# How the softmax denominators reach DRAM and come back: blocks of 32x32 transposed on VectorE, 128-byte rows, and the broadcast and the multiply in later groups

## The chip, the cores and the metric

The kernel runs on one core of one Trainium2 chip. The metric is the device time of one execution in microseconds. Before the change three runs gave 1148.82, 1153.21 and 1153.7 us (median 1153.21).

## The reference

Attention over 4 batches of 8 heads (576 tokens, head size 64), with a threshold in the softmax, then two feed-forward layers over the 2304 tokens:

```python
scores = scale * np.matmul(q, k.transpose(0, 1, 3, 2))
thresh = np.max(scores, axis=-1, keepdims=True) - tau
scores = np.where(scores >= thresh, scores, -1000000000.0)
scores = scores - np.max(scores, axis=-1, keepdims=True)
attn = np.exp(scores)
attn = attn / (np.sum(attn, axis=-1, keepdims=True) + 1e-09)
x = np.matmul(attn, v)                       # to 2304 x 512
h = x @ w_in;   x = (h * sigmoid(1.702 * h)) @ w_out
h = x @ w_in2;  out = (h * np.tanh(softplus(h))) @ w_out2
```

All inputs and the output are float32. `w_in` is 512x2048, `w_out` 2048x512.

## The kernel before

**Stages.** Attention comes first (to about 362 us), then layer 1 and layer 2, which are long rows of TensorE matmuls to the end. A "head" below is a pair of heads (b, hp), 16 of them. Each head is five groups: four "full" ones of 128 query rows for both heads of the pair, and one "mix" group of the last 64 rows of both.

**One group.** `qk` (L599) multiplies queries by keys into the score banks. `softmax_a` does the rest for each half: VectorE scales and takes the row extremum (L621), GpSimd adds the threshold to a 128x1 column `nm` (L625), ScalarE takes the exponential (L628), and VectorE masks it and sums each row into one column of the tile `sm` (L631). Two groups later (AHEAD = 2) `attend` transposes the probabilities on TensorE (L691, and L686 for the tail), ScalarE copies them to SBUF (L702), TensorE multiplies them with the values (L716), and ScalarE copies the product, still without its denominator, into the head's tile `xo` (L723). The L716 matmuls of a mix group are 64 columns wide, those of a full one 128; that is how heads are told apart in the trace.

**The denominators.** After the mix group `scale_x` takes the nine columns of `sm` (128 partitions x 9), inverts them on VectorE (L644), stores them to a DRAM row `r_d` of 1152 numbers in which the partition runs fastest (L645), reads that row back three times, broadcast over 64 partitions each, into the one tile `rb` (L648), multiplies `xo` by `rb` on GpSimd (L654) and stores the result to `x_d` (L656), from where layer 1 loads it. The store and the loads are

```python
dma(lambda: nc.sync.dma_start(out=rd.rearrange("(j q) -> q j", q=128), in_=sums), ...)
dma(lambda: nc.sync.dma_start(out=rb[rows:rows + 64, c0:c0 + m],
    in_=rd[at:at + m].rearrange("(o q) -> o q", o=1).to_broadcast([64, m])), ...)
```

**What sets the order.** Every operation is given to a planner (`Order.add`) with an engine, an estimated duration, the tiles it reads and writes, and a rank. `Order.run` simulates the engines with a list scheduler (lowest rank first among what is ready) and emits the program in the order of the simulated times. So each engine, and SP, which issues all DMAs, runs a fixed order in which every instruction waits for its own data, with all that is behind it waiting too. The planner takes a DMA to need 2.0 us and its bytes at 200 GB/s (L21, L22), whatever its shape. Operations marked `port` on VectorE and GpSimd are planned one at a time.

**Beside it.** From group 40 on (the eighth head of the sixteen has gone by) one block of layer 1's weights is loaded in each head (`sr`, L371 and L375; blocks 0 to 7 in the attention stage, 8 to 15 behind it) and split by `conv_w` and `split_w` into a high and a low part: three ScalarE operations (L380, L382, L400), four on VectorE (L386, L389, L394, L402) and one on GpSimd (L392). Keys and values of coming heads are loaded by L576 and L577 on SP. Layer 1's matmuls are L495 and L540, layer 2's L495 and L885.

Of the kernel before, what the change touches and what calls it, by code (L numbers as in the profile page):

```python
# [11 lines left out]
F32 = mybir.dt.float32  # L12
# [3 lines left out]
ALU = mybir.AluOpType  # L16
# [7 lines left out]
AR = 0.1  # L24
# [9 lines left out]
AHEAD = 2  # L34
# [166 lines left out]
def attention_then_two_ffn_kernel(  # L201
# [21 lines left out]
    nc = tc.nc  # L223
    B, HP, _, S = kq.shape
    S = S // 2
# [88 lines left out]
    def t_tt(n):  # L314
        return 0.15 + n * 2.1e-3

    def dma(fn, nbytes, r=(), w=(), rank=0.0, deps=(), dur=0.47):
        return add("SP", dur, fn, r, w, rank, deps, nbytes)
# [242 lines left out]
    pps = Ring(apool, "p", NP // 2, [128, P1 + S + 1], F32)  # L561
    sss = Ring(apool, "ss", NSS, [128, S + 5], F32)
    nms = Ring(apool, "nm", 4, [128, 2], F32)
    sms = Ring(apool, "sm", 2, [128, 9], F32)
    rbs = Ring(apool, "rb", 1, [128, S], F32)
    pms = Ring(apool, "pm", NPM, [128, 512], F32)
    pmt = Ring(apool, "pmt", 2, [128, 128], F32)
# [2 lines left out]
    sm = {}  # L570
# [36 lines left out]
    def softmax_a(sums, ksum, col, rank, bank, pair, i):  # L607

        s3, ksc = bank
        ns, kns = sss.next()
        at, a = (4, 3) if i == 0 else (P1, P1)
        whole = slice(a, a + S + 1)
        p, kp = pair[0], pair[1] + (i,)
        nm, kn = nms.next()
        n3 = ns[:, 4:4 + S].rearrange("p (g n) -> p g n", g=2)
        scored.append(len(sch.ops))
        add("DVE", t_dve(S) + 0.075,  # L620
            lambda: nc.vector.tensor_scalar(  # L621
                n3, s3, nqsc, None, ALU.mult, ALU.min, accum_out=nm[:, 0:1]),
            ksc, [kn, kns], rank - SMR)
        add("POOL", 0.2,
            lambda: nc.gpsimd.tensor_scalar(nm[:, 1:2], nm[:, 0:1], tau_p, 0.0, ALU.add, ALU.add),  # L625
            [kn, "qsc"], [kn + (1,)], rank - SMR, port=True)
        add("ACT", t_act(S, 1, False),
            lambda: nc.scalar.activation(p[:, at:at + S], ns[:, 4:4 + S], AF.Exp, bias=nm[:, 0:1], scale=-1.0),  # L628
            [kns, kn], [kp], rank)
        add("DVE", t_dve(S) + 0.08,  # L630
            lambda: nc.vector.scalar_tensor_tensor(  # L631
                p[:, whole], ns[:, 3 + i:4 + S + i], nm[:, 1:2], p[:, whole], ALU.is_le, ALU.mult,
                accum_out=sums[:, col:col + 1]),
            [kns, kn, kn + (1,), "qsc"], [kp, ksum + (col,)], rank, port=True)
        return kp

    def scale_x(b, hp, rank):

        sums, ksum = sm[b, hp]
        x, kx = xo[b, hp]  # L640
        rb, krb = rbs.next()
        rd = r_d[b * HP + hp]
        keys = [ksum + (i,) for i in range(9)]
        add("DVE", 0.2, lambda: nc.vector.reciprocal(sums, sums), [], keys, rank)  # L644
        n = dma(lambda: nc.sync.dma_start(out=rd.rearrange("(j q) -> q j", q=128), in_=sums),  # L645
                4608, keys, [("rd", b, hp)], rank)
        for rows, c0, at, m in ((0, 0, 0, S), (64, 0, 640, 512), (64, 512, 576, 64)):
            dma(lambda rows=rows, c0=c0, at=at, m=m: nc.sync.dma_start(  # L648
                out=rb[rows:rows + 64, c0:c0 + m],
                in_=rd[at:at + m].rearrange("(o q) -> o q", o=1).to_broadcast([64, m])),  # L650
                64 * m * 4, [("rd", b, hp)], [krb + (rows + c0,)], rank)
        kr = [krb + (i,) for i in (0, 64, 576)]
        add("POOL", t_tt(S),
            lambda: nc.gpsimd.tensor_tensor(x, x, rb, ALU.mult),  # L654
            kr, [kx + (i,) for i in range(5)], rank, port=True)
        n = dma(lambda: nc.sync.dma_start(out=x_d[1][hp, :, b * S:(b + 1) * S], in_=x),  # L656
                128 * S * 4, [kx + (i,) for i in range(5)], [], rank)
        x_stores.append((n, 1, b * S, (b + 1) * S))

    def attend(tl, ps, pair, rank):  # L660

        kind, b, hp, t = tl
        full = kind == "full"
        _, vr, _, kvr = head[b, hp]
        w = 128 if full else 64
        at = t * 128
        if t == 0:
            xo[b, hp] = xos.next()
        if full:
            plan = [(0, pms, (0, 1), 128, 512), (1, pms, (2, 3), 128, 512), (2, pmt, (4,), 128, 128)]  # L670
        else:
            plan = [(0, pms, (0, 1, 2, 3), 128, 512), (1, pmt, (4,), 64, 128)]
        where, copies, keys = {}, [], []
        for bank, ring, cs, rows, cols in plan:
            pn, kpn = ring.next()
            keys.append(kpn)
            for n, c in enumerate(cs):
                where[c] = (bank, n * 2 * w, pn)
            copies.append((bank, pn, kpn, rows, cols))

        def tr(cs):
            for c in cs:
                bank, c0, _ = where[c]
                if c == 4:
                    m = 64 * len(ps)
                    nc.tensor.transpose(tb[bank][0:m, 0:128], pair[:, 516:516 + m], ident)  # L686
                    yield
                    continue
                for i in range(len(ps)):
                    a = (P1 + 64 if i else 4) + c * 128  # L690
                    nc.tensor.transpose(  # L691
                        tb[bank][:, c0 + i * 128:c0 + (i + 1) * 128], pair[:, a:a + 128], ident)
                    yield

        for (bank, pn, kpn, rows, cols), (*_, cs, _, _) in zip(copies, plan):
            n = 1 if 4 in cs else len(ps) * len(cs)
            n = add("PE", n * 0.109 + (0.16 if bank == 0 else 0.0), lambda cs=cs: tr(cs),
                ps, [("tb", bank)], rank, steps=max(n, 2))
            if sch.fill is None and WARM:
                sch.fill = ("PE", n, 0.107, keep_warm)  # L700
            add("ACT", t_act(cols),
                lambda pn=pn, bank=bank, rows=rows, n=cols: nc.scalar.copy(pn[0:rows, 0:n], tb[bank][0:rows, 0:n]),  # L702
                [("tb", bank)], [kpn], rank)
        i = avn[0] % 2
        avn[0] += 1
        av, kav = tb[3][:, i * 128:i * 128 + w], ("tb", 3, i)

        def mm():
            for c in range(5):
                _, c0, pn = where[c]  # L710
                for i in range(2):
                    rows, at, vc = slice(0, 128), c0 + i * w, c * 128 + 64 * i
                    if c == 4:
                        rows = slice(64 * i, 64 * i + 64) if full else slice(0, 64)
                        at, vc = (0, 512) if full else (64 * i, 512 + 64 * i)
                    nc.tensor.matmul(  # L716
                        av[64 * i:64 * i + 64], vr[rows, vc:vc + 64], pn[rows, at:at + w],
                        start=(c == 0), stop=(c == 4))
                    yield

        add("PE", len(CK) * 0.107 * (2 if full else 1) + 0.2, mm, keys + [kvr], [kav], rank - AR, steps=2 * len(CK))
        x, kx = xo[b, hp]
        add("ACT", t_act(w), lambda: nc.scalar.copy(x[:, at:at + w], av), [kav], [kx + (t,)], rank - AR)  # L723
        if not full:
            scale_x(b, hp, rank - AR)

    avn = [0]


    groups = []  # L730
# [10 lines left out]
    def make_ident():  # L741
        make_identity(nc, ident)
        nc.sync.dma_start(out=tau_b, in_=tau.to_broadcast([128, 1]))
        for t in sss.tiles:
            for c in (3, S + 4):
                nc.vector.memset(t[:, c:c + 1], -3.0e38)
        for t in pps.tiles:
            for c in (3, P1 + S):
                nc.vector.memset(t[:, c:c + 1], 1e-9)
        nc.vector.tensor_scalar_max(tau_p, tau_b, 0.0)  # L750
        nc.vector.tensor_scalar(nqsc, tau_b, 0.0, -scale, ALU.is_ge, ALU.mult)
# [5 lines left out]
    for gi, tl in enumerate(groups + [None] * AHEAD):  # L757
        first = len(sch.ops)
        if tl:
            for bh in preps.get(gi, []):  # L760
                prep(*bh, gi - PR)
            kind, b, hp, t = tl
            if t == 0:
                sm[b, hp] = sms.next()
            sums, ksum = sm[b, hp]
            pair, kpair = pps.next()
            ps = [softmax_a(sums, ksum, 5 * i + t, gi, bank, (pair, kpair), i)
                  for i, bank in enumerate(qk(tl, gi))]
            marks.append(len(sch.ops) - 1)
            behind.append((tl, ps, pair, gi))  # L770
        if gi >= AHEAD:
            attend(*behind.pop(0))
        att.extend(range(first, len(sch.ops)))

    def load_w1_from(fs):
# [197 lines left out]
```

## Time and profile before

| | |
|---|---|
| runs | 1148.82, 1153.21, 1153.7 us |
| profiled execution, own time | 1149.93 us |
| its span, first to last instruction | 1147.7 us |
| mean granted TensorE clock | 0.978 of full speed |
| busy: TensorE, VectorE, ScalarE, GpSimd | 96%, 59%, 57%, 16% of the span |
| DMA, mean over the span | 82 GB/s |

The profile counts an engine as busy while an instruction is on it; a TensorE that counts as busy may run at half its clock, so the granted clock is read beside it. "Idle before" is the time in which an engine had nothing running before an instruction, with the event that ended it behind an arrow.

### The profile page before, as it was taken

Reading aid. Unit: us, or ns where it says so; the run is one execution under the profiler, and the core shown is the slowest. Engines: PE = TensorE matmul, PEld = TensorE weight load, DVE = VectorE, ACT = ScalarE, POOL = GpSimd, SP = SyncE. Lnnn points to the kernel's source line nnn. Section 1 sums busy time; section 2 is a strip of 40 time slices with the busy share of each in tenths; the row PEclk is TensorE's granted clock in tenths of the full one; section 3 lists DMA queues with packets and bytes.
Section 4 is the critical chain, followed back from the end, with each engine's and each line's share of the span. In section 5 each row is a group of like instructions: output and inputs, shape, how many; then the busy total and the mean of one; then the engine's idle time right before and its main releaser. Section 6 shows DMA issues by size and latency. Waiting matters only on the chain.

```text
span 1147.7 us, 17435 instructions
## 1 busy us (share of the span) xinstructions
PE 1102.8 (96%) x6708; PEld 887.9 (77%) x6708; DVE 678.4 (59%) x1336; ACT 651.2 (57%) x1065; POOL 183.4 (16%) x198
## 2 busy tenths in 40 slices
PE   9999998978888999999999999999999999999998
PEld 7667665655656889988888888888888888888887
DVE  7668776777776874554553334456554654554554
ACT  5657666766665644554442234468656656555665
POOL 2323323333433420230320000000000000000000
PEclk9989998989989999999999999999999999999999
DMA  2223414544448434454551033230010010000010
GB/s 86 83 78 94 105 54 123 104 134 91 93 100 166 163 104 145 169 200 147 186 175 44 2 110 106 96 129 1 28 37 1 10 37 1 1 28 10 1 38 18
DMA packets 66690, 94.51 MB, mean 82 GB/s; under 512 B 23856, under 2 KB 41776, under 8 KB 66608
## 3 DMA queue, kind: packets, MB, share of 16 engines
q1 hardware_dynamic: 66608, 93.41, 27.7%
q8 instruction: 52, 0.85, 0.3%
q14 instruction: 30, 0.25, 0.1%
HBM read 70.78 MB, written 22.62 MB: 81 GB/s over the span
## 4 chain that ended last, share of the span: by engine, by line
PE 70%; DMA 6%; DVE 1%; ACT 1%; issue 1%; SPq 0%; POOL 0%; ACTq 0%; DVEq 0%; POOLq 0%
PE h L495 34%; PE tb L885 17%; PE tb L540 17%; DMA sr<-in_w_out 5%; PE sc L599 1%; DMA r_d<-sm 1%; PE tb L716 1%; PE tb L691 0%; DMA sr<-in_w_in 0%; DVE p L631 0%; DVE ss L621 0%; SPq L371 0%; ACT p L628 0%; ACT sr L382 0%; DVE sv L386 0%
## 5 line engine op out<-in xcount | busy, mean ns | idle before, releaser
L847 ACT ACTIVATE ms<-ms 128x512 f32<-128x512 f32 (+1 forms) x240 | 131.1, 583 | 133.8 <-DVE ms L832 132.8
L495 PE MATMUL h<-xa,wh 128*128 128x512 f32 x640 | 198.3, 391 | 0.0
L495 PE MATMUL h<-x,wh 128*128 128x512 f32 (+1 forms) x640 | 165.3, 346 | 0.0
L631 DVE SCALAR_TENSOR_TENSOR p<-ss,nm,p 128x577 f32<-128x577 f32 x144 | 117.9, 837 | 50.4 <-POOL nm L625 36.9
L495 PEld LDWEIGHTS h<-xa,wh 128*128 128x128 f32 x640 | 120.3, 189 | 24.8
L621 DVE TENSOR_SCALAR_CACHE_REDUCE ss<-sc,nqsc 128x576 f32<-128x576 f32 x144 | 112.4, 814 | 35.1 <-PE sc L599 33.2
L628 ACT ACTIVATE p<-ss,nm 128x576 f32<-128x576 f32 x144 | 111.0, 782 | 38.9 <-DVE ss L621 38.5
L495 PEld LDWEIGHTS h<-x,wh 128*128 128x128 f32 x640 | 112.7, 189 | 15.8
L495 PE MATMUL h<-xa,wl 128*128 128x512 f32 x320 | 124.8, 390 | 0.0
L521 ACT ACTIVATE t<-h 128x512 f32<-128x512 f32 (+1 forms) x80 | 44.5, 556 | 140.5 <-PE h L495 140.1
L524 DVE SCALAR_TENSOR_TENSOR h<-t,h 128x512 f32<-128x512 f32 (+1 forms) x80 | 51.3, 641 | 120.4 <-ACT t L521 120.3
L857 DVE TENSOR_TENSOR ms<-ms,hs 128x512 f32<-128x512 f32 (+1 forms) x80 | 50.1, 636 | 122.1 <-ACT ms L847 122.0
L540 PE MATMUL tb<-gh,wh 128*128 128x512 f32 (+1 forms) x320 | 117.9, 369 | 1.0 <-ACT xo L723 1.0
L540 PE MATMUL tb<-gl,wh 128*128 128x512 f32 (+1 forms) x320 | 117.7, 368 | 0.0
L540 PE MATMUL tb<-gh,wl 128*128 128x512 f32 (+1 forms) x320 | 117.7, 368 | 0.0
L599 PE MATMUL sc<-kq 64*128 64x288 f32 (+3 forms) x672 | 108.5, 434 | 5.2 <-DVE ss L621 5.1
L392 POOL TENSOR_TENSOR sv<-sv,sr 128x1024 uint32<-128x1024 uint32 x32 | 82.3, 2573 | 188.1 <-DVE sv L389 100.5
L885 PE MATMUL tb<-wh,g2h 128*128 128x512 f32 x288 | 112.1, 389 | 0.0
L885 PE MATMUL tb<-wl,g2h 128*128 128x512 f32 x288 | 112.1, 389 | 0.0
L885 PE MATMUL tb<-wh,g2l 128*128 128x512 f32 x288 | 112.0, 389 | 0.0
L495 PE MATMUL h<-x,wl 128*128 128x512 f32 (+1 forms) x320 | 110.9, 347 | 0.0
L691 PE MATMUL tb<-ident,p 128*128 128x128 f32 x576 | 91.3, 293 | 20.3 <-DVE p L631 17.9
(57 smaller groups left out, 1757.5 us busy)
## 6 DMA issues: line engine op xcount, KB each, us to landing
sr<-in_w_in SPq DMA_DIRECT2D x32, 512.0 KB, 4.8
sr<-in_w_out SPq DMA_DIRECT2D x32, 512.0 KB, 6.6
kq<-in_kq SPq DMA_DIRECT2D x16, 576.0 KB, 4.2
sv<-x_d SPq DMA_DIRECT2D x16, 512.0 KB, 4.6
w_d<-sv SPq DMA_DIRECT2D x16, 512.0 KB, 5.5
sv<-w_d SPq DMA_DIRECT2D x16, 512.0 KB, 3.5
vr<-in_v SPq DMA_DIRECT2D x16, 320.0 KB, 3.4
x_d<-xo SPq DMA_DIRECT2D x16, 288.0 KB, 2.5
```

The source lines that it names most:

```text
L392: lambda: nc.gpsimd.tensor_tensor(bits, bits, word(0), ALU.add), keys, [kval], rank, port=True)
L495: nc.tensor.matmul(hb[dst][:, 0:n], a[:, c, :], x[:, lo, c, 0:n], start=(i == 0), stop=(i == 3 * KD - 1))
L524: lambda: nc.vector.scalar_tensor_tensor(h(), t()[:, 0:n], 1.0, h(), ALU.add, ALU.mult),
L540: nc.tensor.matmul(accs[e][0][:, 0:n], a[:, es], b()[:, 0:n], start=(f == 0 and i == 0), stop=(f == KF - 1 and i == 2), skip_group_check=True,
L599: nc.tensor.matmul(dst, q, kq2[rows, k0:k0 + n], start=True, stop=True)
L621: lambda: nc.vector.tensor_scalar(n3, s3, nqsc, None, ALU.mult, ALU.min, accum_out=nm[:, 0:1]),
L628: lambda: nc.scalar.activation(p[:, at:at + S], ns[:, 4:4 + S], AF.Exp, bias=nm[:, 0:1], scale=-1.0),
L631: lambda: nc.vector.scalar_tensor_tensor(p[:, whole], ns[:, 3 + i:4 + S + i], nm[:, 1:2], p[:, whole], ALU.is_le, ALU.mult, accum_out=sums ...
L691: nc.tensor.transpose(tb[bank][:, c0 + i * 128:c0 + (i + 1) * 128], pair[:, a:a + 128], ident)
L847: nc.scalar.activation(m()[:, 0:n], m()[:, 0:n], fn, bias=bias)
L857: lambda m=m, hs=hs, n=n: nc.vector.tensor_tensor(m()[:, 0:n], m()[:, 0:n], hs()[:, 0:n], ALU.mult),
L885: nc.tensor.matmul(accs[t][0], x[:, t * 128:(t + 1) * 128], w, start=(f == 0 and i == 0), stop=(f == KF - 1 and i == 2), skip_group_check= ...
```

## The change

`scale_x` gives back three steps instead of adding all of them at once. `invert` inverts the nine columns, transposes the `sm` tile (now 128x32, set to 1.0 once at the start) in 32x32 blocks on VectorE into a new tile `rt`, and issues four stores, one for each block of 32 partitions, of nine rows of 32 numbers (128 bytes) each. `spread` issues the same three broadcast loads in the next group's pass of the loop, `multiply` the GpSimd multiply and the store to `x_d` in the pass after that; both are also told to come after that group's last softmax operation (`marks`). For the last head all three are added in the last pass. The rank of `invert` goes from two groups back to the present group, and the planner's duration of L625 from 0.2 to 0.3.

```diff
-    sms = Ring(apool, "sm", 2, [128, 9], F32)
+    sms = Ring(apool, "sm", 2, [128, 32], F32)
+    rts = Ring(apool, "rt", 1, [128, 32], F32)
...
-        add("POOL", 0.2,
+        add("POOL", 0.3,
             lambda: nc.gpsimd.tensor_scalar(nm[:, 1:2], nm[:, 0:1], tau_p, 0.0, ALU.add, ALU.add),
...
-        add("DVE", 0.2, lambda: nc.vector.reciprocal(sums, sums), [], keys, rank)
-        n = dma(lambda: nc.sync.dma_start(out=rd.rearrange("(j q) -> q j", q=128), in_=sums),
-                4608, keys, [("rd", b, hp)], rank)
...
+        def invert(rank, deps):
+            add("DVE", 0.2, lambda: nc.vector.reciprocal(sums[:, 0:9], sums[:, 0:9]), [], keys, rank)
+            add("DVE", 0.15, lambda: nc.vector.transpose(rt, sums), keys, [krt], rank)
+            for j in range(4):
+                dma(lambda j=j: nc.sync.dma_start(
+                    out=rd.rearrange("(c j q) -> j c q", j=4, q=32)[j], in_=rt[32 * j:32 * j + 9, :]),
+                    1152, [krt], [("rd", b, hp, j)], rank)
+
+        def spread(rank, deps):
+            for rows, c0, at, m in ((0, 0, 0, S), (64, 0, 640, 512), (64, 512, 576, 64)):
+                dma(lambda rows=rows, c0=c0, at=at, m=m: nc.sync.dma_start(
...
+                    [krb + (rows + c0,)], rank, deps, dur=0.6)
+
+        def multiply(rank, deps):
...
+            add("POOL", t_tt(S),
+                lambda: nc.gpsimd.tensor_tensor(x, x, rb, ALU.mult),
+                kr, kxs, rank, deps, port=True)
...
+        return [multiply, spread, invert]
...
-            scale_x(b, hp, rank - AR)
+            scaling.append(scale_x(b, hp))
...
             attend(*behind.pop(0))
+            for todo in list(scaling):
+                todo.pop()(gi - AR, [marks[min(gi, len(marks) - 1)]] if tl else [])
+                if not todo:
+                    scaling.remove(todo)
+        if tl is None and gi == len(groups) + AHEAD - 1:
+            for todo in scaling:
+                while todo:
+                    todo.pop()(gi - AR, [])
```

## Rows read from the trace of the kernel before

**Rows 1.** Page, part 4: the chain that ended last, by engine and by line.

```profile
PE 70%; DMA 6%; DVE 1%; ACT 1%; issue 1%; SPq 0%; POOL 0%; ACTq 0%; DVEq 0%; POOLq 0%
PE h L495 34%; PE tb L885 17%; PE tb L540 17%; DMA sr<-in_w_out 5%; PE sc L599 1%; DMA r_d<-sm 1%; PE tb L716 1%; PE tb L691 0%; DMA sr<-in_w_in 0%; DVE p L631 0%; DVE ss L621 0%; SPq L371 0%; ACT p L628 0%; ACT sr L382 0%; DVE sv L386 0%
```

**Rows 2.** Windows between mix groups' first L716: length, PE PEld DVE ACT POOL, clock, DMA.

```profile
29.29:51.25 21.96, 19.38 (x185) 13.83 (x183) 14.17 (x36) 12.79 (x28) 6.07 (x10) 0.92 0.25 71
...
92.28:109.87 17.59, 17.59 (x185) 12.65 (x183) 14.23 (x36) 12.94 (x29) 6.32 (x10) 1.00 0.50 147
109.87:127.71 17.84, 17.84 (x185) 12.90 (x183) 16.84 (x41) 14.40 (x31) 6.13 (x10) 1.00 0.37 88
...
171.11:194.84 23.73, 19.45 (x172) 13.99 (x170) 15.25 (x38) 14.01 (x28) 9.23 (x11) 0.86 0.38 110
194.84:214.74 19.90, 18.41 (x183) 13.04 (x183) 14.96 (x35) 14.59 (x31) 7.28 (x9) 1.00 0.39 130
...
243.01:261.64 18.63, 16.43 (x177) 11.97 (x175) 17.00 (x40) 14.29 (x29) 7.93 (x9) 1.00 0.48 139
...
309.96:333.23 23.27, 20.71 (x185) 14.31 (x184) 19.71 (x43) 15.71 (x31) 10.99 (x12) 0.86 0.47 86
333.23:362.05 28.82, 24.32 (x197) 18.27 (x195) 17.23 (x36) 16.04 (x31) 6.91 (x8) 0.93 0.59 94
362.05:1147.70 785.65, 780.77 (x3729) 657.50 (x3728) 414.57 (x689) 417.92 (x588) 63.03 (x25) 1.00 0.23 76
```

**Rows 3.** TensorE's timeline: start, length, instructions, idle before; a stall at 75, another at 342.

```profile
61.81 1.09 PE L716 MATMUL tb<-pm,vr 128*64 128x128 f32 x16
...
75.13 0.33 PE L691 MATMUL tb<-ident,p 128*128 128x128 f32 x1
78.28 0.90 PE L691 MATMUL tb<-ident,p 128*128 128x128 f32 x3 [2.82 <-DVE p L631]
79.11 1.98 PE L716 MATMUL tb<-pm,vr 128*64 128x128 f32 x16
...
347.14 0.33 PE L691 MATMUL tb<-ident,p 128*128 128x128 f32 x1 [4.18 <-DVE p L631]
```

**Rows 4.** Who waited for whom, whole span: us in total, times, longest.

```profile
POOL xo L654 <- DMA rb<-r_d: 64.4, 13, 8.7
...
DVE p L631 <- POOL nm L625: 36.9, 22, 6.4
...
ACT sv L380 <- DMA sr<-in_w_out: 26.5, 8, 4.5
```

**Rows 5.** GpSimd's timeline: two multiplies, one in the stall at 75.

```profile
75.69 1.40 POOL L654 TENSOR_TENSOR xo<-xo,rb 128x576 f32<-128x576 f32 x1 [5.33 <-DMA rb<-r_d]
...
95.45 1.42 POOL L654 TENSOR_TENSOR xo<-xo,rb 128x576 f32<-128x576 f32 x1 [1.65 <-ACT pmt L702]
```

**Rows 6.** The waits of SP's own queue.

```profile
SPq L648 <- DMA r_d<-sm: 131.9, 15, 10.5
```

**Rows 7.** SP's timeline of one head: start, length of the issue.

```profile
60.75 0.38 SPq L645 DMA_DIRECT2D r_d<-sm  x1
71.23 2.26 SPq L648 DMA_DIRECT2D rb<-r_d  x3
```

**Rows 8.** The chain that ended last, in order of time: start, length.

```profile
258.67 15.36 DMA sr<-in_w_out
```

**Rows 9.** DMA packets, and issues: count, KB each, median us from issue to landing.

```profile
DMA packets 66690, 94.51 MB, mean 82 GB/s; under 512 B 23856, under 2 KB 41776, under 8 KB 66608
...
out<-o SPq DMA_DIRECT2D x18, 256.0 KB, 2.0
...
tau_b<-in_tau SPq DMA_DIRECT2D x1, 0.5 KB, 2.8
```

**Rows 10.** Groups of instructions to 370 us: busy, mean ns, idle before.

```profile
L631 DVE SCALAR_TENSOR_TENSOR p<-ss,nm,p 128x577 f32<-128x577 f32 x144 | 117.9, 837 | 50.4 <-POOL nm L625 36.9 <-ACT p L628 10.6 <-issue 1.8
...
L644 DVE RECIPROCAL sm<-sm 128x9 f32<-128x9 f32 x16 | 3.4, 212 | 0.3
```

More of the change, by code (lines that the diff above doesn't have):

```diff
@@ L635, in softmax_a, with scale_x @@
         return kp
-    def scale_x(b, hp, rank):
+    def scale_x(b, hp):
         sums, ksum = sm[b, hp]
         x, kx = xo[b, hp]
+        rt, krt = rts.next()
         rb, krb = rbs.next()
@@ L643, in scale_x @@
         keys = [ksum + (i,) for i in range(9)]
-        add("DVE", 0.2, lambda: nc.vector.reciprocal(sums, sums), [], keys, rank)
-        n = dma(lambda: nc.sync.dma_start(out=rd.rearrange("(j q) -> q j", q=128), in_=sums),
-                4608, keys, [("rd", b, hp)], rank)
[L647 to L658, printed above, removed]
+        def invert(rank, deps):
[5 more added lines that the diff above has]
+                    1152, [krt], [("rd", b, hp, j)], rank)
@@ new lines, in spread @@
+        def spread(rank, deps):
+            for rows, c0, at, m in ((0, 0, 0, S), (64, 0, 640, 512), (64, 512, 576, 64)):
+                dma(lambda rows=rows, c0=c0, at=at, m=m: nc.sync.dma_start(
+                    out=rb[rows:rows + 64, c0:c0 + m],
+                    in_=rd[at:at + m].rearrange("(o q) -> o q", o=1).to_broadcast([64, m])),
+                    64 * m * 4, [("rd", b, hp, j) for j in range(4)],
+                    [krb + (rows + c0,)], rank, deps, dur=0.6)
+        def multiply(rank, deps):
+            kr = [krb + (i,) for i in (0, 64, 576)]
+            kxs = [kx + (i,) for i in range(5)]
+            add("POOL", t_tt(S),
+                lambda: nc.gpsimd.tensor_tensor(x, x, rb, ALU.mult),
+                kr, kxs, rank, deps, port=True)
+            n = dma(lambda: nc.sync.dma_start(out=x_d[1][hp, :, b * S:(b + 1) * S], in_=x),
+                    128 * S * 4, kxs, [], rank)
+            x_stores.append((n, 1, b * S, (b + 1) * S))
@@ L724, in attend @@
         if not full:
-            scale_x(b, hp, rank - AR)
+            scaling.append(scale_x(b, hp))
     avn = [0]
+    scaling = []
     groups = []
@@ L743, in make_ident @@
         nc.sync.dma_start(out=tau_b, in_=tau.to_broadcast([128, 1]))
+        for t in sms.tiles:
+            nc.vector.memset(t, 1.0)
         for t in sss.tiles:
```

## The prediction

> **What bounds the kernel now.** I read the chain that ended last first. TensorE holds 70% of it, nearly all in the two feed-forward layers (L495, L540, L885), and DMA holds 6%: loads of layer 1's weights and the store of the inverted sums [rows 1]. DMA has no place in a chain that TensorE should set, so the question is where these pieces sit. They all lie in the attention stage. From the last mix group on, 785.65 us run at a clock of 1.00 with TensorE busy for 780.77 [rows 2]; the change touches nothing there.
>
> So I cut the attention stage at the mix groups, one head to a window [rows 2]. A head can take 17.59 or 17.84 us, with TensorE busy from end to end at full clock. Others take 22 to 28. From 29.29 to 171.11, before any weights are converted, seven heads take 141.82 us; the next seven, to 333.23, take 162.12. The granted clock falls to 0.86 in the long heads; the 1.00 of the good ones is the 2.4 GHz level, and the missing part is time at 1.2.
>
> TensorE's timeline shows the loss [rows 3]: in the head at 61.81 it stands 2.82 us for VectorE's masking and then runs sixteen value matmuls in 1.98 us that took 1.09 before. A stall is paid twice, once in idle time and once at the lower level behind it.
>
> Who is late? VectorE waits for GpSimd's 128x1 addition for 36.9 us, and GpSimd's multiply waits for the broadcast rows for 64.4 [rows 4]. In the stall at 75 GpSimd has stood for 5.33 us in front of the multiply [rows 5], with the additions of the next halves behind it. The broadcast loads themselves are late because SP holds them for the store: 131.9 us in 15 waits [rows 6]. In that head the store is issued at 60.75 and the first load at 71.23, 10.5 us later, for 4.5 KB [rows 7]. A store of 256 KB of whole rows lands in 2.0 [rows 9]. Of the packets, 23856 are under 512 bytes [rows 9]; 16 stores of 1152 single numbers make 18432 of them. The same store delays what is issued after it: a weight load takes 15.36 us in the chain [rows 8], and ScalarE, which runs in order, waits 26.5 us for these loads [rows 4] with the probability copies queued behind.
>
> **The change, part by part.**
>
> *The store.* 1152 pieces of 4 bytes become four DMAs of nine pieces of 128 bytes. Its landing is the main unknown. Below: 2.0 us, the fastest store in the trace; above: 10.5, as now. I take 3, since the nearest row by number and size of pieces is the load of tau to 128 partitions, 0.5 KB in 2.8 us [rows 9]. Issues cost 0.38 us each [rows 7], so three more hold SP for 1.1 us a head, and the fourth store lands about 4.5 us after the first issue. SP was standing there for 131.9/15 = 8.8 us; the issues are hidden in that, and without that cover would delay the loads of keys and values by 1.1 us, which the planner ranks two groups ahead of their use.
>
> *The deferred loads.* `spread` comes one group later, 17.6/5 = 3.5 us. SP's wait falls from 8.8 us to about 1, and what is queued behind it (values, keys, weights, the store of `xo`) goes out at its time. At the upper bound the wait would be 10.5 + 1.1 - 3.5 = 8 us.
>
> *The deferred multiply.* It comes one group after the loads. From the first load's issue at 71.23 to the multiply at 75.69 are 4.5 us [rows 5, 7] against 3.5 of a group, so GpSimd may still stand for about 1 us. The multiply at 95.45 waited 1.65 us [rows 5] and lies in the head of 17.59 us without a TensorE stall, so that much is hidden. Its own 1.4 us stay, and the additions behind it wait as they do in that head. The tile `xo` is free again about 2 x 3.5 + 1.4 + 3 = 11 us after the denominators (3 for its store, an estimate as above); in the head at 60.75 it takes 75.69 - 60.75 + 1.4 + 3 = 19 us [rows 5, 7], so the next user of it gains slack.
>
> *VectorE.* One transpose of 128x32 more a head. Below it can't be less than nothing; above, the masking of 128x577 takes 0.84 us [rows 10]. I take 0.2, as the reciprocal on 128x9 takes 0.212 [rows 10], 3.2 us over 16 heads. In a head without weights VectorE is busy 14.23 of 17.59 us and hides it; in one with weights it is busy 17.00 of 18.63 [rows 2], and eight such heads could show 1.6 us. The memsets, done once, lie beside the wait for tau; the 0.1 us that the planner adds to L625 moves no work and costs nothing while TensorE is the last to finish. The reciprocal's later rank delays it by one or two VectorE operations, inside the group that `spread` now leaves free.
>
> *The sum.* The seven heads without weights go to the 17.7 of the two undisturbed ones: 141.82 - 123.9 = 17.9 us. The heads with weights have no row quite free of stalls; the two at full clock took 19.90 and 18.63 [rows 2], and I take their mean, 19.3, since a conversion puts two ScalarE operations ahead of a copy that TensorE needs: 162.12 - 135.1 = 27.0 us. The last head has one stall of 4.18 us [rows 3] in 28.82, but layer 1's matmuls already fill a part of it; I take 3. Together 47.9. The profiled execution took 1149.93 (span 1147.7 and 2.2 around it), so 1102; the median of the runs shown is 3.3 above that execution and the lowest run 1.1 below it, so I say 1103.
>
> Layer 1 then starts some 48 us earlier. Half of its weight blocks are loaded in the attention stage, group by group, and move along; the other half has 43 us of matmuls ahead of it. I cost this at nothing; if conversions lag, layer 1 pays.
>
> **The rivals.**
>
> *VectorE and ScalarE become the bound in the heads with weights.* Speaking for it: the stalls gave conversions room, and 17.00 of 18.63 is close. Against it: the same windows hold a whole conversion. If these heads only come to 21.5, the gain is 17.9 + (162.12 - 150.5) + 1 = 30.5, and the time 1119.
>
> *Half of each wait comes back at the multiply.* The loads' 4.5 us don't fit in one group, and GpSimd stands long enough in some heads to hold VectorE and drop the clock. Half of the gain gives 1126.
>
> *The pieces are not what the store waits for.* Then each of the four stores still takes about 10.5 us, side by side. SP waits 8 us instead of 8.8 and the multiply comes as late as now: 1148, no change. Against it stand the 18432 packets and the 2.0 us of a store 57 times as large. Of the Trainium skill, the page DMA: Bandwidth & Descriptors (Anatomy of one DMA) speaks for this rival: it puts a DMA's time down to about 2 us for the confirmed landing and says that many descriptors can go out before generating them costs much; by that the old store would have landed in about 2 us, so the trace does not agree, but if the landing at this DRAM row is what is slow, the new shape buys nothing.
>
> *Slower: the four stores go one behind the other.* Place: the SP queue's wait in front of `spread`. Price: four times 10.5 is 42 us a head against 17.6 of TensorE work, so a head takes about 46 us and 16 of them put 16 x (46 - 22.5) = 376 us on top: 1526. It decides from the point where all four land later than about 14 us (10.5 and the group that `spread` waits anyway); each microsecond beyond that costs 16 us. Stores of 256 KB landing in 2.0 us speak against it.
>
> **How the numbers follow.** Forecast 1103: 62%. VectorE and ScalarE the bound, 1119: 22%. Half comes back, 1126: 9%. No change: 4%. Slower: 3%. A difference under 0.5%, 5.8 us, can't be told from none here. Faster is then 0.93, same 0.04, slower 0.03. The lower end is every head at 17.7 us: 17.9 + 38.2 + 4 = 60, so 1090, and 1 us for the runs' spread below the profile: 1089. The upper end takes in the first two rivals and 3 us for the runs above the profile: 1129.
>
> **What would show it.** Right: packets under 512 bytes fall to about 23856 - 18432 + 576 = 6000; SP's wait for `r_d` falls from 131.9 us to under 20; the multiply's wait from 64.4 to under 25; weight loads leave the chain; the heads without weights take 17.6 to 17.9 us at a clock of 1.00, and the mix group of the eighth comes at about 153 us instead of 171; layer 1 and 2 keep their 785 us. Wrong: heads with weights over 21 us with VectorE busy throughout, the stores landing in over 5 us, or a new TensorE wait inside layer 1 for a weight block.

## The result and the profile after

The changed kernel takes 1097.09 us (median of 4 runs, 1096.73 to 1097.17) against 1153.34 (1148.82 to 1153.7): a ratio of 0.952, 95% interval 0.9497 to 0.9544. The forecast was 1103, with a range of 1089 to 1129. The profiled execution took 1097.12 us, with a span of 1095.3 against 1147.7.

The chain that ended last, of the kernel after, by engine and by line (PE is TensorE, DVE VectorE, ACT ScalarE, POOL GpSimd; it answers to [rows 1]):

```profile
PE 97%; ACT 1%; DVE 1%; issue 0%; POOL 0%; POOLq 0%; DVEq 0%; ACTq 0%
PE h L495 36%; PE tb L540 18%; PE tb L911 18%; PE tb L731 9%; PE sc L600 8%; PE tb L706 7%; PE tb L701 1%; PE tb L506 0%; DVE p L632 0%; DVE ss L622 0%; ACT p L629 0%; POOL nm L626 0%; ACT pm L717 0%; ACT xo L738 0%; ACT sv L380 0%
```

TensorE's share rose from 70% to 97%; the weight loads and the store of the sums are gone from the chain, and the attention stage's own matmuls (L600, L706, L731) stand in their place.

The windows between the mix groups' first value matmuls, of the kernel after, with the columns of [rows 2] (the second window holds two heads, because the third head's mix group came early in it):

```profile
29.22:46.81 17.59, 17.59 (x186) 12.64 (x184) 14.76 (x36) 12.54 (x28) 6.09 (x10) 1.00 0.28 87
46.81:87.13 40.32, 38.61 (x368) 27.35 (x367) 30.27 (x77) 26.00 (x56) 13.04 (x20) 0.96 0.24 77
...
139.09:158.72 19.63, 19.63 (x199) 14.22 (x197) 18.32 (x47) 14.64 (x32) 7.71 (x12) 1.00 0.40 117
...
178.58:196.51 17.93, 17.93 (x180) 12.76 (x179) 17.77 (x40) 15.48 (x30) 8.39 (x11) 1.00 0.34 105
...
250.42:268.04 17.62, 17.62 (x185) 12.65 (x183) 17.02 (x40) 15.58 (x32) 10.09 (x11) 1.00 0.44 134
268.04:286.44 18.40, 18.07 (x185) 12.98 (x183) 18.29 (x44) 15.58 (x31) 9.79 (x12) 1.00 0.32 111
286.44:1095.30 808.86, 803.20 (x3923) 674.80 (x3923) 439.33 (x732) 434.93 (x621) 77.65 (x33) 1.00 0.23 78
```

The seven heads without weights end at 158.72: 129.50 us against 141.82. The next seven take 286.44 - 158.72 = 127.72 against 162.12. What follows, the last head and both layers, takes 808.86 against 1147.70 - 333.23 = 814.47. That is 12.3 + 34.4 + 5.6, and 0.1 in front of it: the 52.4 us by which the span fell.

The waits of SP's own queue (us in total, times, longest; it answers to [rows 6]), then VectorE's transpose beside the reciprocal in the groups to 320 us, its masking over the whole span (it answers to [rows 10]), and the packets:

```profile
SPq L657 <- DMA r_d<-rt: 9.4, 3, 5.2
```

```profile
L648 DVE RECIPROCAL sm<-sm 128x9 f32<-128x9 f32 x16 | 3.4, 212 | 0.3
L649 DVE STREAM_TRANSPOSE rt<-sm 128x32 f32<-128x32 f32 x16 | 3.3, 208 | 0.2
```

```profile
L632 DVE SCALAR_TENSOR_TENSOR p<-ss,nm,p 128x577 f32<-128x577 f32 x144 | 130.0, 926 | 8.1 <-ACT p L629 6.4
```

```profile
DMA packets 49156, 94.53 MB, mean 86 GB/s; under 512 B 6320, under 2 KB 24240, under 8 KB 49072
```

SP's wait for the store fell from 131.9 us to 9.4. The multiply's wait for its rows, 64.4 us before [rows 4], is not in the list any more, nor are ScalarE's 26.5 us for weights. VectorE stands 8.1 us in front of its masking, where it stood 50.4, and none of that is for GpSimd's addition now. The transpose takes 208 ns; the masking itself takes 926 ns on the mean against 837, which is 12 us more in total. In one case, from 37.61 us, it takes 1.71 us while GpSimd's multiply runs from 37.29 to 38.71.

Of the windows above only one is left with a granted clock under 1.00. TensorE's timeline of the kernel after from 62 us, and the operation for which VectorE stood:

```profile
62.03 1.24 PE L600 MATMUL sc<-kq 64*128 64x288 f32 x8
64.18 1.97 PE L600 MATMUL sc<-kq 64*128 64x288 f32 x8 [0.91 <-DVE ss L622]
66.08 0.33 PE L706 MATMUL tb<-ident,p 128*128 128x128 f32 x1
66.85 1.51 PE L706 MATMUL tb<-ident,p 128*128 128x128 f32 x7 [0.44 <-DVE p L632]
```

```profile
63.30 0.82 DVE L622 TENSOR_SCALAR_CACHE_REDUCE ss<-sc,nqsc 128x576 f32<-128x576 f32 x1 [5.63 <-PE sc L600]
```

Here the planner has put the values of three groups one behind the other, and VectorE, without scores, stood 5.63 us. TensorE's two waits are short, 0.91 and 0.44 us, but it runs at its lower level for some microseconds behind them (eight score matmuls take 1.97 us that took 1.24), which is the 0.96 of that window. It belongs to this order of the instructions: from 40 to 100 us the granted clock is 0.97 here and 1.00 in three kernels below in which the planner wrote another order, the store alone with either of the planner's numbers and the changed kernel with 0.2.

### The profile page after: what moved, and what is told of

Read it like the earlier page. It is cut to its first block, busy times and chain, and to the rows that moved or that the text cites. A ratio compares the mean times of both kernels' runs of the same rounds, so it can differ in the third digit from the quotient of the medians.

```text
span 1095.3 us, 17534 instructions
## 1 busy us (share of the span) xinstructions
PE 1084.9 (99%) x6708; PEld 877.5 (80%) x6708; DVE 692.8 (63%) x1354; ACT 651.2 (59%) x1065; POOL 196.4 (18%) x198
## 2 busy tenths in 40 slices
DMA packets 49156, 94.53 MB, mean 86 GB/s; under 512 B 6320, under 2 KB 24240, under 8 KB 49072
## 4 chain that ended last, share of the span: by engine, by line
PE 97%; ACT 1%; DVE 1%; issue 0%; POOL 0%; POOLq 0%; DVEq 0%; ACTq 0%
PE h L495 36%; PE tb L540 18%; PE tb L911 18%; PE tb L731 9%; PE sc L600 8%; PE tb L706 7%; PE tb L701 1%; PE tb L506 0%; DVE p L632 0%; DVE ss L622 0%; ACT p L629 0%; POOL nm L626 0%; ACT pm L717 0%; ACT xo L738 0%; ACT sv L380 0%
## 5 line engine op out<-in xcount | busy, mean ns | idle before, releaser
L632 DVE SCALAR_TENSOR_TENSOR p<-ss,nm,p 128x577 f32<-128x577 f32 x144 | 130.0, 926 | 8.1 <-ACT p L629 6.4
L629 ACT ACTIVATE p<-ss,nm 128x576 f32<-128x576 f32 x144 | 111.5, 785 | 37.9 <-DVE ss L622 37.4
L626 POOL TENSOR_SCALAR nm<-nm,tau_p 128x1 f32<-128x1 f32 x144 | 88.0, 612 | 168.0 <-DVE ss L622 163.6
L600 PE MATMUL sc<-kq 64*128 64x288 f32 (+3 forms) x672 | 105.0, 417 | 1.0 <-DVE ss L622 0.9
```

Source lines behind the costliest of these rows:

```text
L600: nc.tensor.matmul(dst, q, kq2[rows, k0:k0 + n], start=True, stop=True)
L632: lambda: nc.vector.scalar_tensor_tensor(p[:, whole], ns[:, 3 + i:4 + S + i], nm[:, 1:2], p[:, whole], ALU.is_le, ALU.mult, accum_out=sums ...
```

## The experiments

Theory A is the prediction's: the old store's late landing held SP and, through the loads, GpSimd and TensorE. Theory B: the deferral pays. Theory C: the planner's new order pays.

**The store alone.** The kernel before, with

```diff
+        add("DVE", 0.15, lambda: nc.vector.transpose(rt, sums), keys, [krt], rank)
-        n = dma(... out=rd.rearrange("(j q) -> q j", q=128), in_=sums), ...
+        for j in range(4):
+            dma(... out=rd.rearrange("(c j q) -> j c q", j=4, q=32)[j], in_=rt[32 * j:32 * j + 9, :]), ...
```

> The kernel before with the new store alone (32x32 transposes, four stores of 128-byte rows); the loads and the multiply follow at once as before, and the planner's 0.2 for L625 stays. Theory A (the store's landing is what held SP and GpSimd): SP's wait for r_d falls from 131.9 us to under 50, the multiply's wait from 64.4 to under 30, and most of the gain is here: 1100 to 1112 us. Theory B (the deferral is what pays, since any wait at the multiply holds GpSimd): less than half of the gain, over 1125 us. Theory C (the gain is the new order that the planner happens to write): anything, with the waits not in step with the time.

Measured: 1097.09 us (ratio to the kernel before 0.9514, interval 0.95 to 0.9528), the same as the whole change. SP's timeline of one head (SPq is a DMA that SP issues), and SP's wait:

```profile
56.52 1.35 SPq L649 DMA_DIRECT2D r_d<-rt  x4
58.89 1.73 SPq L653 DMA_DIRECT2D rb<-r_d  x3
```

```profile
SPq L653 <- DMA r_d<-rt: 8.0, 10, 2.7
```

From the first store's issue to the first load's are 2.37 us, where the old store took 10.5 [rows 7]; the fourth store thus landed within about 1.4 us of its issue. The longest of SP's ten waits for the stores is 2.7 us. All of the gain is here, with nothing deferred.

**The deferral alone.** The changed kernel, with

```diff
-            add("DVE", 0.15, lambda: nc.vector.transpose(rt, sums), keys, [krt], rank)
-            for j in range(4): ...
+            dma(lambda: nc.sync.dma_start(out=rd.rearrange("(j q) -> q j", q=128), in_=sums[:, 0:9]),
+                4608, keys, [("rd", b, hp, j) for j in range(4)], rank)
```

> The changed kernel with the old store: one DMA of 1152 single numbers, no transpose, but the loads and the multiply one and two groups later. Theory A: SP still waits about 10.5 - 3.5 = 7 us a head at the loads, weight and key loads behind it stay late, TensorE's clock stays under 1.00 in the attention stage: 1125 to 1145 us. Theory B: the multiply finds its rows in time in most heads: under 1112 us.

Measured: 1138.51 us (0.9861, 0.9814 to 0.9908; single runs from 1128.97 to 1141.44), in theory A's range. SP's wait:

```profile
SPq L654 <- DMA r_d<-sm: 37.4, 6, 9.1
```

So the deferral, with its ranks and the planner's 0.3, takes SP's wait from 131.9 us to 37.4 and brings some 14 us of the 56 while the store is slow. Theory A has the time right and the wait wrong: it had SP still stand 7 us a head, over 100 in all. That most of the wait goes, and little of the time with it, suggests that the old store does harm beyond being waited for.

**The planner told the truth.** The kernel before, with

```diff
-                4608, keys, [("rd", b, hp)], rank)
+                1600000, keys, [("rd", b, hp)], rank)
```

> The kernel before with one number of the planner's changed: the old store is planned as 1.6 MB, that is 2.0 + 8.0 us, which is about what it takes; the instructions are the same, their order is planned anew. Theory A: the planner then moves the multiply behind other GpSimd work by itself, so GpSimd's wait falls, but SP and the loads behind the store still stand: 1115 to 1140 us. Theory B (it is only GpSimd's place in the order): about 1100 to 1110. Theory C: no better than the kernel before.

Measured: 1133.4 us (0.9823, 0.98 to 0.9846), theory A's range, and again not by theory A's way, which had SP still stand. SP's wait for the store is 13.9 us here, about as little as after the change, and the time is still 36 us longer. The wait is not all.

**An extra old store.** The changed kernel with a store of the old shape to a DRAM row that nobody reads:

```diff
+            dma(lambda: nc.sync.dma_start(out=junk[b * HP + hp].rearrange("(j q) -> q j", q=128), in_=sums[:, 0:9]),
+                0, keys, [("junk", b, hp)], rank)
```

> The changed kernel with one more store a head: the nine columns in the old shape (1152 single numbers) into a DRAM row that nobody reads; nothing waits for it but the tile's next use two heads later. Theory A with contention (the many small pieces also delay the DMAs behind them on the queue): the broadcast loads land some 7 us later, the multiply waits again, 1110 to 1135 us. Theory A without contention (only the wait for the store's end costs): 1097 to 1100 us.

Measured: 1139.99 us (0.9897, 0.9866 to 0.9928): 43 us are lost again, more than either reading allowed. The planner issued it in front of the four new stores, so SP waited 28.1 us for those; that left open whether the place in the queue did it.

**Four old stores in place of one.** The kernel before, with

```diff
+        for j in range(4):
+            dma(... out=rd.rearrange("(c j q) -> j q c", j=4, q=32)[j], in_=sums[32 * j:32 * j + 32, :]), ...
```

> The kernel before with its store cut into four, each of 32 partitions x 9 single numbers (288 pieces of 4 bytes); no transpose, nothing deferred. If the number of pieces sets the landing (theory A), the four together still take about 10 us, SP's wait stays near 130 us and the time within 10 us of the kernel before. If a DMA's shape or its being one DMA sets it, the four land side by side in a few microseconds and the time falls towards 1097.

Measured: 1158.56 us (1.0051, 1.003 to 1.0073), a little slower than before. SP's timeline:

```profile
63.02 1.82 SPq L646 DMA_DIRECT2D r_d<-sm  x4
74.63 1.79 SPq L650 DMA_DIRECT2D rb<-r_d  x3
```

11.6 us to the first load. Four DMAs are no remedy by themselves; it is the shape of the pieces.

**The extra old store on another queue.** As above, but issued by ScalarE and planned at no time, so that the order of all else is that of the changed kernel:

```diff
+            add("ACT", 0.0, lambda: nc.scalar.dma_start(
+                out=junk[b * HP + hp].rearrange("(j q) -> q j", q=128), in_=sums[:, 0:9]), ...
```

> The changed kernel with one more store a head of 1152 single numbers to a DRAM row that nobody reads, issued by ScalarE on its own queue and planned at no time, so that the order of all other instructions stays. If the old store harms by standing in the same queue in front of other transfers, this costs little: 1097 to 1105 us, of which 16 issues on ScalarE are some. If it harms by holding the DMA engines or the DRAM themselves, the transfers of SP's queue are late too: 1115 to 1140.

Measured: 1146.39 us (0.9944, 0.9923 to 0.9965). The idea that the store harms only what stands behind it in its queue falls: in another queue it costs 49 us. Its sixteen issues hold ScalarE for 0.38 us each, 6 us at most. DMA's busy share in 40 slices of 0.05 us from 41 to 43 us (a digit is tenths), and the packets by queue (q10 is ScalarE's):

```profile
DMA  0159777777777777101000000010000000279898
...
q10 hardware_dynamic: 1168, 0.00, 26.4%
q1 hardware_dynamic: 113, 0.10, 14.8%
```

The DMA engines are through with the 1168 packets in 0.8 us. But the store of `xo`, which SP issues at 41.91 us, is held up: packets of this kernel from 44 to 52 us, then of the changed kernel from 43 to 47:

```profile
DMA packets 23, 0.03 MB, mean 4 GB/s; under 512 B 8, under 2 KB 8, under 8 KB 23
```

```profile
DMA packets 6, 0.00 MB, mean 0 GB/s; under 512 B 6, under 2 KB 6, under 8 KB 6
```

Of its 128 rows of 2304 bytes eighteen take 1.3 to 6.9 us each, and the last goes out at 50.8 us; in the changed kernel none takes over 0.12 us, and all are out by 43.1. Two views of the same kernel at that time, VectorE's, then ScalarE's timeline:

```profile
50.60 0.82 DVE L623 TENSOR_SCALAR_CACHE_REDUCE ss<-sc,nqsc 128x576 f32<-128x576 f32 x1 [3.91 <-remote]
```

```profile
51.61 0.21 ACT L743 COPY xo<-tb 128x64 f32<-128x64 f32 x1 [4.00 <-remote]
```

Both engines stand for 4 us, GpSimd for 4.8 and TensorE for 2.6 with them, without a releaser that the profile names. What the trace keeps of the semaphores tells a little more. VectorE's operation at 50.60 waits for TensorE's scores of 46.19 to 47.43, and TensorE's semaphore is recorded as raised only at 50.58. Of ScalarE's 982 updates 35 are not recorded at all, none between 46.1 and 51.8 us. All kernels here that write single numbers to DRAM lack such records, and none of the others does. So "<-remote" is no wait for nothing: the engines stood for each other's signals, and the one that can be followed here came 3 us after the work.

**The same extra store behind the four stores, and behind the loads, on SP.** The order of all else is kept by issuing it in the same step as the fourth store, or as the third load:

```diff
-                dma(lambda j=j: nc.sync.dma_start(...rt...),
+                dma(lambda j=j: (nc.sync.dma_start(...rt...), old_store() if j == 3 else None),
```

This is the first of the two; the second has `old_store() if m == 64` at the loads.

> The same extra store on SP, issued together with the fourth new store and behind it, order of all else unchanged. The four stores that are waited for go ahead of it; behind it in the queue are the store of xo, the load of values and, a group later, the broadcast loads. Queue theory: the loads, 7 us later, come out of it a few us late and the keys and weights behind: 1105 to 1130 us, less than the 1140 of the run with the extra store in front of the four. Wait theory (only a wait for the old store itself costs): 1097 to 1100.

> The same extra store on SP, issued together with the third broadcast load and behind it, order unchanged. Now only transfers with slack (keys of a later head, weights) and the next head's four stores come behind it, these some 9 us later. Queue theory: the smallest loss of the three, 1097 to 1110 us, and more in the heads with weights than in those without. If DMA engines or DRAM are what is held, as large a loss as behind the stores.

Measured: 1146.85 us (0.9958, 0.9936 to 0.9981) and 1122.14 us (0.9747, 0.9705 to 0.9789). Both beyond what the queue theory gave; behind the loads the loss is half as large, 25 us. But there the store is waited for, as the waits of VectorE show:

```profile
DVE p L633 <- DMA junk_d<-sm: 23.4, 8, 7.9
```

The extra store reads `sm`, and so late in the head it still holds that tile when VectorE's masking wants to write to it. How much this kernel would lose without that wait, no run shows. In the kernel with the store behind the four, no compute engine waits for it, and SP does once, for 1.4 us.

**A load of the same shape.** In the place behind the four stores, 1152 single numbers are read from the DRAM row of the head before, into a tile that nobody reads:

```diff
+                nc.sync.dma_start(out=back, in_=r_d[b * HP + hp - 1].rearrange("(j q) -> q j", q=128))
```

> The changed kernel with, behind the four new stores of a head, a load in the old shape in place of the extra store: 1152 single numbers of the head before, read from its DRAM row into a tile that nobody reads (15 loads); order of all else unchanged. If it is the number of pieces alone that holds the DMA engines, as large a loss as with the extra store at that place: 1135 to 1150 us. If it is small writes to DRAM that are slow, this costs less than half of that: 1097 to 1118 us.

Measured: 1097.2 us (0.9519, 0.9502 to 0.9536), no loss at all. DMA packets from 40 to 160 us of this kernel, then of the one with the extra store at the same place:

```profile
DMA packets 13933, 11.35 MB, mean 95 GB/s; under 512 B 9694, under 2 KB 10206, under 8 KB 13919
```

```profile
DMA packets 11519, 9.17 MB, mean 76 GB/s; under 512 B 8294, under 2 KB 8294, under 8 KB 11505
```

The window of the fast kernel holds more heads, but over the whole span too it has nearly as many packets under 512 bytes, 23840 against 25008, and it is as fast as without them. So the number of pieces by itself doesn't do it; of reads and writes of single numbers in DRAM, it is the writes.

**The same bytes in 128 rows.** Against the kernel with the extra store behind the four:

```diff
-            ...out=junk[b * HP + hp].rearrange("(j q) -> q j", q=128), in_=sums[:, 0:9])
+            ...out=junk[b * HP + hp].rearrange("(q j) -> q j", j=9), in_=sums[:, 0:9])
```

> The changed kernel with the extra store at the same place and of the same 4.5 KB, but as 128 rows of 36 bytes instead of 1152 single numbers. If the cost goes with the number of pieces, a ninth of the loss of 50 us: 1097 to 1107 us. If any store of small rows that misses the DRAM's own width is slow, most of it stays: 1120 us and more.

Measured: 1097.47 us (0.952, 0.9506 to 0.9534). DMA's busy share from 41 to 57 us in slices of 0.4 us, first of the kernel with the 1152 single writes, then of this one:

```profile
DMA  0000489900080010530030303010100094796551
```

```profile
DMA  0000139500000000000085897571000000958971
```

In both, the stores and the 288 KB of `xo` go out at about 42.6. Here they are over by 44.2. With the single writes, lone packets go on until 53 us (14 rows of 2304 bytes among them, the size of the rows of `xo`), and the next loads come 5 us later.

**The planner's 0.2 in the changed kernel, and 0.3 with the store alone.**

```diff
-        add("POOL", 0.3,
+        add("POOL", 0.2,
```

This is the first of the two; the second is the kernel with the store alone and 0.3 in place of 0.2.

> The changed kernel with the planner's 0.2 us for L625's operation instead of 0.3: only the order is planned anew. The term was put at nothing: 1092 to 1103 us, within 0.5% of 1097. More than that would mean that part of the gain is the order that the planner happens to write.

> The kernel before with the new store and the planner's 0.3 for L625, nothing deferred. Beside the store-only run (1097.09) and the changed kernel (1097.09) it shows what the deferral itself is worth at the same planner constants: within 0.5%, 1092 to 1103 us, if the deferral is worth nothing once the store is quick; over 1103 if the deferral repairs something that the 0.2 only hid by chance.

Measured: 1095.65 us (0.9505, 0.949 to 0.9521) and 1094.91 us (0.95, 0.9486 to 0.9515). With 0.2 the deferral takes the store-only kernel from 1097.09 to 1095.65, with 0.3 from 1094.91 to 1097.09: once a gain of 1.4 us and once a loss of 2.2, both under the 5.8 that count here. The last kernel, the new store without the deferral, is the lowest of all and its runs (1094.37 to 1095.87) lie below those of the changed kernel, but by 0.2% only.

## Why the prediction was right, point by point

**The bound and the cause** were right: the gain lies in the attention stage, it comes from the store's shape, and the store-only kernel has all of it. The no-change rival (the pieces don't matter) and the slower one (four stores one behind the other) are out: the four new stores land side by side, the last within 1.4 us of its issue.

**The store's landing** was put at 3 us, with 2.0 as the least, and the set of four at 4.5 from the first issue. In the head shown the last landed 1.4 us after its issue, under that least, and the set took 2.37. It is not always so: in the changed kernel SP once waits 5.2 us for the stores, to 277.1 us in a head with weights, which is past the 5 us that was named as a sign of being wrong. TensorE stands only 0.33 us in that window.

**The deferral** stood in the sum as the step that brings SP's wait from 8.8 us to 1 and lets the multiply find its rows. That step was not needed: without it SP waits ten times, 0.8 us on the mean. With the quick store the deferral is worth nothing measurable; with the old one it brought 14 us.

**The terms of the sum.** 17.9 us for the heads without weights measured 12.3: they did not all reach 17.7, since the order around 62 us cost a stall and the eighth mix group came at 158.7 instead of 153. 27.0 for the heads with weights measured 34.4: their 19.3 came from two windows in which TensorE still stood 1.5 and 2.2 us [rows 2]; heads with weights now take 18.2 on average. The rival that VectorE becomes the bound is out at its 21.5 us a head, but not by far: in the windows above VectorE is busy 17.77 of 17.93 us and 18.29 of 18.40, and in the latter TensorE stands 0.33. In such heads it has next to nothing left. The last head was put at 3 and layer 1 at nothing; together they gave 5.6. One error of 5.6 us too much and two of 7.4 and 2.6 too little left 47.9 against 52.4 in the span; that the sum came so close is in part luck. The rest of the 56.2 between the medians is that the runs before lie above their profile by 3.4 us and those after don't.

**VectorE's transpose** was put at 0.2 us and took 0.208. **Packets** under 512 bytes: 6320 instead of 6000. The trace has 18 for each of the 64 new stores, nine rows and nine packets of 4 bytes, and 1168 for an old one, 16 more than its numbers: 64 x 9 - 16 x 16 = 320.

**What the prediction had only half.** It explained the old store's 10 us by the work on its 1152 pieces and the damage by what waits for it or stands behind it in SP's queue. A view of the kernel before that I had not read speaks against the first: DMA's busy share from 60 to 72 us in slices of 0.3 us, around the store issued at 60.75.

```profile
DMA  9300037600000000000000000000000000000200
...
DMA packets 1218, 0.18 MB, mean 15 GB/s; under 512 B 1184, under 2 KB 1184, under 8 KB 1216
```

The packets are out by 62.4 us; then nothing moves, and the store counts as landed at 71.2. So 9 us lie behind the last packet; what happens in them no view shows. The extra stores speak against the second: on ScalarE's queue, and on SP's behind the four, they do their harm unread, with next to no wait for them. The Trainium skill's page DMA: Bandwidth & Descriptors (Anatomy of one DMA, which is written for DMAs that GpSimd issues) says that most of a DMA's fixed cost is the confirmation of the last write and that it can be surprisingly long when the target is HBM. The trace agrees with the place, not with the size: the page gives about 2 us, and here, for a store that SP issues, it is 9.

**What stays open.** Which part of the memory path holds the single writes is not settled, nor why the engines' signals come late while they drain. Two rivals stand untested. The old layout has 128 partitions write side by side into the same 512 bytes of DRAM, so the harm may come of the neighbours and not of the 4 bytes; single numbers far apart were not tried. And since records of the trace itself are missing at these times, it may be the recording that is held up and holds the engines; every run here has a recorded span, so none shows the kernel without it.

## What to carry to other kernels

A store whose rows in DRAM are single 4-byte numbers should be turned first, even if it is only 4.5 KB and nobody waits for it: a 32x32 transpose of 0.2 us and rows of 128 bytes did it here. An extra store in rows of 36 bytes did no harm either, but nobody waited for it, so its landing is not known. Look at the DMA's busy share beside the landing: if the packets are out and the landing is still far, the time is not in the store's own packets, and here neither another queue (49 us lost) nor a place behind the stores that were waited for (50) helped. Change the shape before the order; the deferral that looked like half of this change was worth nothing once the store was quick. And before an extra store is called unwaited for, look at who waits for the tile that it reads: in one run here that was VectorE.

## What the runs showed of the hardware that was not expected

- 1152 single 4-byte writes to DRAM, side by side over the partitions, leave the DMA engines in about 0.8 us and count as landed some 9 us after; 128 writes of 36 bytes, the same 4.5 KB, cost the kernel nothing (1097.47 against 1097.09), and neither do 1152 single reads (1097.20). Rows of 36 bytes are far below the 512 bytes that the Trainium skill gives as the least for full rate (DMA: Bandwidth & Descriptors, Specifications); at these sizes no run here shows a cost of that.
- Such a store slows a transfer of another queue: with it on ScalarE's queue, rows of 2304 bytes of a store on SP's take up to 6.9 us each, where none takes over 0.12 without it. Sixteen of them cost 49 us, about as much as the whole change had gained.
- While it drains, a signal from TensorE to VectorE is recorded 3 us after the work (50.58 against 47.43), and the trace lacks some of its own records of such signals.
